# Both layers of a gated feed-forward block from split operands on the full array

## The chip, the cores and the metric

The kernel runs on one core of a Trainium2 chip. The metric is the device time of one execution in microseconds (us). One execution is also profiled: its trace gives the start and end of each instruction on the engines: TensorE (PE, with its weight loads PEld), VectorE (DVE), ScalarE (ACT), GpSimd (POOL), and the queues that issue DMAs (SP, and the queues of ACT and POOL).

## The reference

A causal convolution along the tokens with seven taps (the weights of a head, after a softmax over the taps, are shared by its 24 channels), then a feed-forward block with a hard-swish gate:

```python
B, S, D = 8, 4096, 192          # n_heads 8, kernel_size 7, d_ff 2048
w = softmax(weight, axis=-1)    # 8 x 7
x_pad = concatenate([zeros((B, 6, D)), x], axis=1)
y[b, s, h*24 + g] = sum_k w[h, k] * x_pad[b, s + k, h*24 + g]
h = y @ w_in                    # 32768 x 192 @ 192 x 2048
g = h * clip(h + 3, 0, 6) / 6
out = g @ w_out                 # 32768 x 2048 @ 2048 x 192
```

Both weight matrices arrive as 64-bit numbers and are rounded to fp32 on the chip. The input x arrives transposed, channels ahead of tokens.

## The kernel before, in words

The 32768 tokens are worked in 32 blocks of 1024, each as two halves of 512 tokens. d_ff is cut in 16 chunks of 128.

**Layout.** The 192 channels lie as three pieces (`K3`) of 64 rows. Partitions 0 to 63 hold the first 512 tokens of a block, 64 to 127 the second 512. A matmul of the first layer so uses half of the array's rows, and two of them, one per half, run side by side. w_in lies the same way, chunks 0 to 7 on the lower partitions and 8 to 15 on the upper ones. So that each token half also meets the other half's chunks, y is swapped between the partition halves by DMAs on SP (`swap`, `swap_parts`, L266/L267, six for each block).

**First layer.** Block 0 runs in plain fp32 (`half_mm`, L296). From block 1 on, `first_layer` (`mms`, L508 and L516) runs in the type float32r (f32r) on split operands: a number is cut by `high_of` and `from_high` into a high part and a rest, both short enough for that type, and a third part (MIX) that mixes both. For each of 16 (group, chunk) pairs it sums HIGH x HIGH and LOW x LOW in PSUM, has ACT multiply the sum by 4097 (L528), and adds MIX x MIX: 18 half-array matmuls of 512 columns, in nine pairs side by side. ACT's relu (L302) and DVE's gate (L306) then form g in SBUF.

**Second layer.** `second_layer` writes out a schedule by hand: four streams of matmuls, one per strip of 32 array columns, run side by side in fp32 (L623). It uses a seven-product scheme on 2 x 2 blocks (token half by d_ff half, d_ff half by output half), for one strip with a second level of the same scheme. This needs sums of parts of g: by DVE and POOL (`g_sums` L412, `small_sums` L586, L456), and by accumulating DMAs on POOL's queue (L565). Products are put together in PSUM and SBUF by ACT copies and DVE additions; DVE transposes 32 x 32 blocks (L462) and SP stores 32 columns at a time (L372, twelve DMAs of 64 KB a block).

**Side work.** `conv_jobs` does the taps of the block after next on ACT (first tap, L927) and DVE (L929), 1536 columns at a time; L474, L945 and L477 split y.

**Start.** `Rounding` turns 64-bit words into fp32 in units of 128 x 384: DVE takes exponent and mantissa out (`split`, L171, L175), ACT clamps (`clamp`, L183, L186, L189), DVE joins (`join`, L192, L196), POOL multiplies (L200). There are 16 units, eight for each layer. In block 0 they are interleaved with the first layer's relus and gates; the second layer of block 0 (`out_direct`, L341) runs as plain fp32 sums.

The order on each engine is the program's (`tc.manual_schedule()`); the semaphores follow from the tiles.

Of the kernel before, what the change touches and what calls it, by code (L numbers as in the profile page):

```python
# [18 lines left out]

CUT = 1.0 - 2.0**-13  # L20
EPS = 2.0**-12
HIGH, LOW, MIX = range(3)
# [3 lines left out]
def kernel(  # L26
# [17 lines left out]
    G = 2  # L44
    TB = G * N
    D2 = P // 2
    K3 = D // D2
    GJ = GS // K3
    NC = DFF // P
    NT = TB // P  # L50
    BPB = S // TB
    NB = B * BPB
    assert H * GJ == D2 and K3 * GJ == GS and G == 2 and S % TB == 0 and DFF % P == 0 and PAD <= N

    NP = NC // 2
    DH = D // 2
    QS = 32
    NQ = DH // QS
    assert NQ * QS == DH and NQ == 3 and P // QS == 4

    cst = ctx.enter_context(tc.tile_pool(name="cst", bufs=1))
    xs = ctx.enter_context(tc.tile_pool(name="xs", bufs=1))
    ys = ctx.enter_context(tc.tile_pool(name="ys", bufs=1))
    ot = ctx.enter_context(tc.tile_pool(name="ot", bufs=1))
    ps = ctx.enter_context(tc.tile_pool(name="ps", bufs=1, space=bass.MemoryType.PSUM))
    start_pools, first_in = ExitStack(), ExitStack()
    stg = start_pools.enter_context(tc.tile_pool(name="stg", bufs=8))
    cnv = start_pools.enter_context(tc.tile_pool(name="cnv", bufs=4))
    fi = first_in.enter_context(tc.tile_pool(name="fi", bufs=1, side="right"))

    def x_source(i):
        b, t0 = i // BPB, (i % BPB) * TB
        src = xT[b].rearrange("(p s) t -> p s t", s=K3)
        head = PAD if t0 == 0 else 0
        return head, src[..., t0 - PAD + head : t0 + N], src[..., t0 + N - PAD : t0 + TB]

    def load_x(i, dma=nc.sync):
        x = xs.tile([P, K3, PAD + N], F32, name="x")
        head, lower, upper = x_source(i)
        if head:  # L80
            nc.vector.memset(x[0:D2, :, 0:PAD], 0.0)
        dma.dma_start(out=x[0:D2, :, head:], in_=lower)
        dma.dma_start(out=x[D2:P, :, :], in_=upper)
        return x


    w_sb = cst.tile([P, KC], F32, name="w_sb")
    for base, dma in ((0, nc.scalar), (D2, nc.sync)):
        dma.dma_start(  # L89
            out=w_sb[base : base + D2],  # L90
            in_=weight.unsqueeze(1).to_broadcast([H, GJ, KC]),
        )


    x_tiles = {0: xs.tile([P, K3, PAD + N], F32, name="x")}
    nc.vector.memset(x_tiles[0][0:D2, :, 0:PAD], 0.0)

    def load_x0(s, dma_lower, dma_upper):
        head, lower, upper = x_source(0)
        dma_lower.dma_start(out=x_tiles[0][0:D2, s, head:], in_=lower[:, s])  # L100
        dma_upper.dma_start(out=x_tiles[0][D2:P, s, :], in_=upper[:, s])

    load_x0(K3 - 1, nc.gpsimd, nc.gpsimd)
    load_x0(0, nc.sync, nc.scalar)

# [4 lines left out]
    zeros = cnv.tile([P, N], F32, name="zeros", bufs=1)  # L110
    nc.vector.memset(zeros[:], 0.0)


    w_in = fi.tile([P, NP, K3, P], F32, name="w_in")


    w_out = cst.tile([P, NP, 7, DH], F32, name="w_out")
    B11, B12, B21, B22, T1, T2, T4 = range(7)
    T3 = B12
    w_s = cst.tile([P, 2, 4, NP // 2, QS], F32, name="w_s")  # L120

    w_in_bits = moe_w_in.bitcast(U32).rearrange("(p s) (c f w) -> c p s f w", s=K3, f=P, w=2)
    w_out_bits = moe_w_out.bitcast(U32).rearrange("(k c p) w -> p c k w", p=P, k=2)
    WS = K3 * P
    assert 2 * D == WS
# [4 lines left out]
    def load_w_in(j):  # L130
        st = stage()
        for half in range(2):
            nc.sync.dma_start(  # L133
                out=st[half * D2 : (half + 1) * D2].rearrange("p (s f) w -> p s (f w)", s=K3),
                in_=w_in_bits[j + half * NP].rearrange("p s f w -> p s (f w)"),
            )
        return st

    def load_w_out(j):
        st = stage()  # L140
        nc.sync.dma_start(
            out=st[:].rearrange("p (k d) w -> p k (d w)", k=2), in_=w_out_bits[:, j]
        )
        return st

# [5 lines left out]

    class Rounding:

        def __init__(self, load, dst):  # L160
            self.load_words, self.dst = load, dst

        def load(self):
            self.st = self.load_words()

        def split(self):
            high = self.st[:, :, 1]
            self.top = cnv.tile([P, WS], U32, name="top")
            self.scale = cnv.tile([P, WS], U32, name="scale")
            self.sig = cnv.tile([P, WS], F32, name="sig")  # L170
            nc.vector.tensor_scalar(  # L171
                out=self.scale[:], in0=high, scalar1=0x7FF00000, scalar2=None,
                op0=ALU.bitwise_and,
            )
            nc.vector.tensor_scalar(  # L175
                out=self.top[:], in0=high, scalar1=0xFFFFF, scalar2=0x100000,
                op0=ALU.bitwise_and, op1=ALU.bitwise_or,
            )

        def clamp(self):  # L180


            nc.scalar.activation(  # L183
                self.sig[:], self.scale[:], ACT.Relu, bias=bias_e[:, 0:1], scale=-1.0
            )
            nc.scalar.activation(  # L186
                self.scale[:], self.sig[:], ACT.Relu, bias=bias_e[:, 1:2], scale=-8.0
            )
            nc.scalar.mul(self.sig[:], self.st[:, :, 0], 2.0**-52)  # L189

        def join(self):
            nc.vector.scalar_tensor_tensor(  # L192
                out=self.scale[:], in0=self.st[:, :, 1], scalar=0x80000000,
                in1=self.scale[:], op0=ALU.bitwise_and, op1=ALU.bitwise_or,
            )
            nc.vector.scalar_tensor_tensor(  # L196
                out=self.sig[:], in0=self.top[:], scalar=2.0**-20, in1=self.sig[:],
# [3 lines left out]
                out=self.dst, in0=self.sig[:], in1=self.scale[:].bitcast(F32), op=ALU.mult  # L201
            )
    def w_in_unit(j):
        return Rounding(lambda: load_w_in(j), w_in[:, j].rearrange("p s f -> p (s f)"))

    def w_out_unit(j):
        dst = w_out[:, j, B11 : B22 + 1].rearrange("p b d -> p (b d)")
        return Rounding(lambda: load_w_out(j), dst)

    def w_sums(sums):  # L210
        for o, x, y in sums:
            nc.vector.tensor_tensor(
                out=w_out[:, :, o], in0=w_out[:, :, x], in1=w_out[:, :, y], op=ALU.subtract
            )

    units = [w_in_unit(j) for j in range(NP)] + [w_out_unit(j) for j in range(NP)]
    AHEAD = 4
    for n in range(AHEAD):
        units[n].load()
        if n == 0:  # L220
            load_x0(1, nc.sync, nc.sync)

    mx = cst.tile([P, 1], F32, name="mx")
    nc.vector.tensor_reduce(out=mx[:], in_=w_sb[:], axis=AX.X, op=ALU.max)
    e_sb = cst.tile([P, KC], F32, name="e_sb")
    nc.vector.tensor_tensor(
        out=e_sb[:], in0=w_sb[:], in1=mx[:].to_broadcast([P, KC]), op=ALU.subtract
    )
    nc.scalar.activation(e_sb[:], e_sb[:], ACT.Exp)
# [96 lines left out]

# [694 lines left out]
```

## Time and profile before

| what | us |
|---|---|
| three runs, median (lowest to highest) | 2230.66 (2230.26 to 2230.84) |
| span of the profiled execution, first to last instruction | 2228.3 |
| median less that span | 2.4 |
| TensorE busy | 2221.0 |
| DVE, ACT, POOL busy | 1894.3, 1379.2, 823.6 |
| fp32 matmuls of the second layer (L623) on g and w_out | 967.5 busy, 552 ns each |
| f32r matmuls of the first layer (L516), two groups | 524.9 and 516.1 busy, 388 and 386 ns each |
| gates (L306), 128 x 1024 | 598.0 busy, 1219 ns each |
| relus (L302), 128 x 1024 | 545.3 busy, 1113 ns each |

The profiled execution is known by its span; the three timed runs are other executions. Matmuls overlap, so the busy time of a group is less than count times mean, and a busy TensorE does not mean a full array. An fp32 matmul shows as two records (two passes), an f32r matmul as one. In the rows quoted below, `64*128` is rows by columns of the array that are in use, and the tile names say which operand is read.

### The profile page before, as it was taken

The page shows a single profiled execution, that of the slowest core. Times are in us where ns is not written, and L with a number is a line of the kernel's source. Part 1 is how long each engine was busy: PE and PEld are TensorE (multiplying, and loading weights), DVE is VectorE, ACT ScalarE, POOL GpSimd, SP SyncE. Part 2 cuts the span into 40 slices and gives each one's busy share as a digit, 9 for nine tenths or more (in the row PEclk, how much of TensorE's full clock was granted, in tenths as well). Part 3 has the DMA queues.
Part 4 walks back from the last instruction along what each step waited for, and adds up shares of the span by engine and source line. Part 5 has one row for each costly group of instructions (what it writes and reads, how often), then busy time and mean ns, then how long its engine had stood idle before and what let it go on. Part 6 is the DMA issues. An engine that isn't in the chain of part 4 may idle for free.

```text
span 2228.3 us, 50401 instructions
## 1 busy us (share of the span) xinstructions
PE 2221.0 (100%) x21527; PEld 1560.8 (70%) x21527; DVE 1894.3 (85%) x1673; ACT 1379.2 (62%) x1678; POOL 823.6 (37%) x690
## 2 busy tenths in 40 slices
PE   9999999999999999999999999999999999999999
PEld 5477776677766777766777667786677776677766
DVE  8888888888888888888888888888888888888876
ACT  7457665576655676555766557665567655576654
POOL 2344432344422444223443234442244422344323
PEclk9999999999999999999999999999999999999999
DMA  6244224443244342344422443324434234442232
GB/s 157 58 98 84 49 58 91 85 83 63 53 82 91 77 80 46 71 91 84 84 48 58 91 87 81 67 49 82 91 78 82 47 67 91 84 84 52 55 77 34
DMA packets 253584, 166.58 MB, mean 75 GB/s; under 512 B 208016, under 2 KB 213136, under 8 KB 253360
## 3 DMA queue, kind: packets, MB, share of 16 engines
q1 hardware_dynamic: 234872, 129.46, 28.4%
q0 software_dynamic: 17248, 33.64, 8.7%
q8 instruction: 169, 2.77, 0.5%
q10 hardware_dynamic: 1240, 0.27, 0.1%
q14 instruction: 55, 0.45, 0.1%
HBM read 31.72 MB, written 25.17 MB: 26 GB/s over the span
## 4 chain that ended last, share of the span: by engine, by line
PE 99%; DMA 0%; DVE 0%; SPq 0%; ACT 0%; issue 0%; DVEq 0%; ACTq 0%
PE psum L623 49%; PE psum L516 46%; PE psum L296 2%; PE psum L341 2%; PE psum L508 0%; DMA x<-in_x_dram 0%; SPq L100 0%; SPq L133 0%; DVE top L175 0%; PE psum L824 0%; DVE y L255 0%; DVE results L456 0%; SPq L89 0%; ACT y L838 0%; ACT scale L186 0%
## 5 line engine op out<-in xcount | busy, mean ns | idle before, releaser
L623 PE MATMUL psum<-g,w_out 128*32 128x512 f32 (+1 forms) x6712 | 967.5, 552 | 0.0
L306 DVE SCALAR_TENSOR_TENSOR g<-g,psum 128x1024 f32<-128x1024 f32 (+1 forms) x528 | 618.3, 1186 | 203.6 <-ACT g L302 203.1
L586 POOL TENSOR_TENSOR s<-g 128x256 f32<-128x256 f32 x248 | 273.9, 1104 | 1244.4 <-DVE g L306 1244.4
L302 ACT ACTIVATE g<-psum,half 128x1024 f32<-128x1024 f32 (+1 forms) x528 | 564.8, 1086 | 4.9 <-PE psum L516 0.3
L623 PEld LDWEIGHTS psum<-g,w_out 128*32 128x32 f32 x6712 | 371.7, 110 | 246.0 <-issue 126.7
L516 PE MATMUL psum<-y,w_in 64*128 64x512 f32 x4464 | 524.9, 388 | 0.0
L516 PE MATMUL psum<-y_other,w_in 64*128 64x512 f32 x4464 | 516.1, 386 | 0.0
L528 ACT ACTIVATE psum<-psum 128x1024 f32<-128x1024 f32 x465 | 469.0, 1009 | 54.4 <-PE psum L516 52.1
L516 PEld LDWEIGHTS psum<-y,w_in 64*128 64x128 f32 x4464 | 435.4, 184 | 71.2 <-ACT psum L528 0.3
L516 PEld LDWEIGHTS psum<-y_other,w_in 64*128 64x128 f32 x4464 | 423.8, 184 | 82.1
L623 PE MATMUL psum<-s,w_out 128*32 128x512 f32 (+1 forms) x3272 | 465.5, 570 | 0.0
L929 DVE SCALAR_TENSOR_TENSOR y<-x,c_sb,y 128x1536 f32<-128x1536 f32 x186 | 335.3, 1803 | 2.6 <-ACT y L927 1.4
L412 POOL TENSOR_TENSOR s<-g 128x1024 f32<-128x1024 f32 x93 | 285.8, 3073 | 26.7 <-DVE g L306 26.5
L623 PE MATMUL psum<-g,w_s 128*32 128x256 f32 x1240 | 282.8, 379 | 0.0
L623 PEld LDWEIGHTS psum<-s,w_out 128*32 128x32 f32 x3272 | 154.3, 110 | 81.8 <-issue 49.4
L623 PEld LDWEIGHTS psum<-g,w_s 128*32 128x32 f32 x1240 | 136.4, 110 | 67.7
L412 DVE TENSOR_TENSOR s<-g 128x2048 f32<-128x2048 f32 (+1 forms) x93 | 181.3, 1977 | 1.1
L623 PE MATMUL psum<-s,w_s 128*32 128x256 f32 x744 | 170.7, 379 | 0.0
L586 DVE TENSOR_TENSOR g<-g 128x1024 f32<-128x1024 f32 x124 | 151.7, 1224 | 5.2
L412 DVE TENSOR_TENSOR g<-g 128x2048 f32<-128x2048 f32 x62 | 139.0, 2284 | 0.0
L620 ACT COPY psum<-psum 32x512 f32<-32x512 f32 x93 | 51.3, 551 | 135.4 <-PE psum L623 135.4
L456 DVE TENSOR_TENSOR results<-psum,results 32x256 f32<-32x256 f32 (+3 forms) x128 | 69.3, 541 | 50.9 <-issue 45.5
(93 smaller groups left out, 1316.6 us busy)
## 6 DMA issues: line engine op xcount, KB each, us to landing
y_other<-y SPq DMA_DIRECT2D x186, 384.0 KB, 5.1
g<-g POOLq DMA_DIRECT2D x62, 512.0 KB, 5.0
out_dram<-results SPq DMA_DIRECT2D x378, 64.0 KB, 2.0
x<-in_x_dram SPq DMA_DIRECT2D x53, 388.5 KB, 7.7
stage<-in_moe_w_in_dram SPq DMA_DIRECT2D x16, 192.0 KB, 4.8
stage<-in_moe_w_out_dram SPq DMA_DIRECT2D x8, 384.0 KB, 5.5
x<-in_x_dram SPq DMA_DIRECT2D x7, 384.0 KB, 8.3
x<-in_x_dram POOLq DMA_DIRECT2D x2, 388.5 KB, 5.3
```

The source lines that it names most:

```text
L296: nc.tensor.matmul(out=psum[:, b], lhsT=w[r], rhs=src, start=start, stop=stop, skip_group_check=onto,)
L302: nc.scalar.activation(r6, h, ACT.Relu, bias=half[:], scale=1.0 / 6.0)
L306: nc.vector.scalar_tensor_tensor(out=g_, in0=g_, scalar=1.0, in1=h, op0=ALU.min, op1=ALU.mult)
L341: lambda p=p: nc.tensor.matmul(out=bank[j * QS : (j + 1) * QS, tokens], lhsT=w_out[:, p, w, cols], rhs=x[:, p, tokens], start=(first and p ...
L412: engine.tensor_tensor(out=o[:, r], in0=a[:, r], in1=b[:, r], op=op)
L456: nc.vector.tensor_tensor(out=out, in0=x, in1=y, op=op)
L516: nc.tensor.matmul(out=psum[:, 2 * slots[n] + k], lhsT=r32(w_in_parts[part][r, c, s]), rhs=r32(y_other[0][r, part, s] if group else y_own[ ...
L528: nc.scalar.mul(both(n), both(n), 4097.0)
L586: engine.tensor_tensor(out=o, in0=p, in1=q, op=op)
L620: streams[3].append((t - 0.5, lambda: fn(*args, **kw)))
L623: nc.tensor.matmul(out=out, lhsT=w, rhs=x, start=start, stop=True, tile_position=(0, j * QS), skip_group_check=True,)
L929: jobs.append(lambda k=k: nc.vector.scalar_tensor_tensor(out=y[:], in0=x[:, :, k : k + N], scalar=c_sb[:, k : k + 1], in1=y[:], op0=ALU.mu ...
```

## The change

Both layers now run in f32r on operands split in two parts that this type holds exactly, a high part and the rest, with all products summed straight in PSUM. There is no scaling between the products, no seven-product scheme, and no fp32 matmul but seven for the convolution of block 0.

- Layout: 128 of the 192 channels (16 of each head) fill all partitions for 1024 tokens (part a). The other 64 channels (part b) lie in both partition halves, one token half each.
- First layer of a chunk: for part b, high x low weight on half the rows, two side by side (`first_rows`); then four full-array matmuls per token half (`first`): part b's high and low parts stacked on 128 rows, and part a's high x high, high x low weight, low x full weight.
- Second layer of a chunk (`second`): three products on g's high part and two on its low part, for each token half: ten full-array matmuls. One of them holds 64 columns of high weights and 64 of low ones, so that its two row halves are added at the store.
- Order: chunks go in pairs. In each block TensorE does the first layer of pair p, then the second layer of pair p - 1. After relu and gate, ACT copies g's high part and DVE subtracts it for the low part.
- Start: sixteen units, of 512 columns for the first layer and 384 for the second. Besides the rounding, each also makes high and low parts (`parts_of`, ACT and POOL). The two units of pair p + 1 are placed behind pair p's work in block 0.
- Gone: the swaps of y, the sums of g, the accumulating DMAs, and the additions between products.

The diff, cut to the core of the new code:

```diff
+    def parts_of(sig, high, lows):
+        nc.scalar.mul(r32(high), sig, CUT)
+        for to, src, top in lows:
+            nc.gpsimd.tensor_tensor(out=r32(to), in0=src, in1=top, op=ALU.subtract)
+
+    def in_unit(j):
+        high, low = (w1[:, n, j].rearrange("p a c f -> p (a c f)") for n in range(2))
+
+        def finish(sig):
+            parts_of(sig, high, [(low, sig, high)])
+            nc.scalar.copy(
+                out=r32(w1_full[:, j].rearrange("p c f -> p (c f)")), in_=sig[:, 0 : 2 * P]
+            )
+            nc.scalar.copy(out=r32(high[D2:P, 2 * P :]), in_=sig[D2:P, 2 * P :])
...
+    def matmul(out, w, x, start, stop, position=(0, 0)):
+        nc.tensor.matmul(
+            out=out, lhsT=r32(w), rhs=r32(x), start=start, stop=stop,
+            tile_position=position, skip_group_check=True,
+        )
+
+    def first_rows(c, yp):
+        for k, b in enumerate(banks_of(c)):
+            matmul(
+                psum[:, b], w1[rows[k], LOW, c // 2, 1, c % 2], yp[3][rows[k]],
+                True, False, (k * D2, 0),
+            )
+
+    def first(c, yp):
...
+        steps = (
+            (w1[:, HIGH, c // 2, 1, c % 2], 2), (w1[:, HIGH, c // 2, 0, c % 2], HIGH),
+            (w1[:, LOW, c // 2, 0, c % 2], HIGH), (w1_full[:, c // 2, c % 2], LOW),
+        )
+        for k, b in enumerate(banks_of(c)):
+            for n, (w, x) in enumerate(steps):
+                matmul(psum[:, b], w, yp[x][:, halves[k]], False, n == len(steps) - 1)
+
+    def second(p, parts):
...
+        for c in range(2):
+            w = w2[:, 2 * p + c]
+            jobs += [(0, w[:, 0], high, c), (0, w[:, 2], high, c), (2, w[:, 1], high, c)]
+        for c in range(2):
+            ch = 2 * p + c
+            jobs += [(0, w2_full[:, ch], low, c), (2, w2[:, ch, 1], low, c)]
...
+    def store(i):
...
+        for k in range(2):
+            nc.scalar.copy(out=upper[rows[k]], in_=psum[rows[1 - k], SUMS + 2 + k])
+        xts = [ot.tile([P, N], F32, name="xt") for _ in range(3)]
+        for k in range(2):
+            nc.vector.transpose(out=xts[k][:], in_=psum[:, SUMS + k])
+        for k in range(2):
+            nc.vector.tensor_tensor(
+                out=sums[rows[k]], in0=psum[rows[k], SUMS + 2 + k], in1=upper[rows[k]],
+                op=ALU.add,
+            )
+        nc.vector.transpose(out=xts[2][:], in_=sums[:])
...
+    def unit_step(n):
+        if n < len(units):
+            units[n].split()
+            units[n].clamp()
+            units[n].join()
+            units[n].part()
+        if n + AHEAD < len(units):
+            units[n + AHEAD].load(nc.sync)
...
+            for p in range(NP):
+                parts = new_g()
+                pair = 2 * p, 2 * p + 1
+                for c in pair:
+                    first_rows(c, yp)
+                for c in pair:
+                    first(c, yp)
+                if finished is not None:
+                    store(finished)
+                    finished = None
+                for c in pair:
+                    relu_of(c, parts)
+                for c in pair:
+                    gate_of(c, parts)
+                for c in pair:
+                    g_high(c, parts)
+                for c in pair:
+                    g_low(c, parts, nc.vector)
+                if last is not None:
+                    second(*last)
+                    if last[0] == NP - 1:
+                        finished = i - 1
+                last = p, parts
+                if i == 0:
+                    unit_step(2 * p + 2)
+                    unit_step(2 * p + 3)
...
+                if more:
+                    if p == 0:
+                        tap(xn, 0, 0, nc.scalar)
+                        tap(xn, 1, 0, nc.scalar)
+                    for part, k in taps[2 * p : 2 * p + 2]:
+                        tap(xn, part, k, nc.vector)
+                    if p == NP - 2:
+                        yn = new_y()
+                        split_a(yn)
+                        split_b(yn)
```

In the changed kernel the helper's matmuls stand at L309 and L310, the copy that waits for POOL at L209, the relu at L360, the gate at L368, the high part at L374, the low part at L378, and the store's DMAs at L384.

## The prediction

> **What bounds the kernel now.** I read the page's busy shares and its chain first, then stages (busy time by windows), then the order in time on TensorE inside one block, then single groups by shape, then the start.
>
> The page:
> ```profile
> span 2228.3 us, 50401 instructions
> PE 2221.0 (100%) x21527; PEld 1560.8 (70%) x21527; DVE 1894.3 (85%) x1673; ACT 1379.2 (62%) x1678; POOL 823.6 (37%) x690
> ...
> PE 99%; DMA 0%; DVE 0%; SPq 0%; ACT 0%; issue 0%; DVEq 0%; ACTq 0%
> PE psum L623 49%; PE psum L516 46%; PE psum L296 2%; PE psum L341 2%; PE psum L508 0%; DMA x<-in_x_dram 0%; SPq L100 0%; SPq L133 0%; DVE top L175 0%; PE psum L824 0%; DVE y L255 0%; DVE results L456 0%; SPq L89 0%; ACT y L838 0%; ACT scale L186 0%
> ```
> TensorE is the whole chain: the second layer (L623) 49%, the first (L516) 46%. Only matmul slots, or a stall that opens between them, can move the time.
>
> Stages (columns: window, its length, busy time of PE, PEld, DVE, ACT, POOL, granted clock, DMA share, GB/s):
> ```profile
> 0.00:99.70 99.70, 97.64 (x600) 44.76 (x600) 87.95 (x149) 61.10 (x98) 29.44 (x34) 1.00 0.43 101
> 99.70:168.20 68.50, 68.50 (x677) 53.46 (x673) 58.65 (x48) 42.09 (x50) 27.07 (x22) 1.00 0.52 107
> 1058.50:1127.00 68.50, 68.50 (x674) 48.55 (x673) 59.02 (x49) 42.64 (x51) 25.64 (x21) 1.00 0.38 74
> ```
> Block 0 lasts 99.7 us, then come 31 blocks of 68.49 (L508 starts every block), and 5.4 at the end: 99.7 + 2123.2 + 5.4 = 2228.3. The clock is 1.00 throughout.
>
> TensorE in order of time (start, length):
> ```profile
> 1058.56 0.38 PE L508 MATMUL psum<-y,w_in 64*128 64x256 f32 x1
> 1058.57 16.09 PE L516 MATMUL psum<-y,w_in 64*128 64x512 f32 x138
> 1074.49 1.52 PE L516 MATMUL psum<-y_other,w_in 64*128 64x512 f32 x12
> ...
> 1076.53 15.12 PE L516 MATMUL psum<-y_other,w_in 64*128 64x512 f32 x132
> 1091.58 6.64 PE L623 MATMUL psum<-g,w_out 128*32 128x512 f32 x63
> ```
> The first layer takes 33.0 us, the second 35.5. The 66 pairs of half-array f32r matmuls in the x132 row take 15.12 - 0.16 = 14.96 us: **226.7 ns a pair**. (One record lasts 386 ns, 0.16 us beyond the next pair's start.)
>
> Two other spacings, an fp32 pass of 256 columns and the full array in fp32:
> ```profile
> 2222.06 0.38 PE L623 MATMUL psum<-g,w_out 128*32 128x256 f32 x1
> 2222.27 0.38 PE L623 MATMUL psum<-g,w_out 128*32 128x256 f32 x1
> 2222.49 0.38 PE L623 MATMUL psum<-g,w_out 128*32 128x256 f32 x1
> ```
> ```profile
> 6.17 7.14 PE L824 MATMUL psum<-x,diag 128*128 128x512 f32 x16
> ```
> A 256-column pass comes every 0.215 to 0.216 us; a 512-column pass on the full array every 0.43 (7.14 less a tail of 0.59 and a first gap of 0.53, over 14).
>
> The price of the weight conversion:
> ```profile
> 9.98 0.60 ACT L183 ACTIVATE sig<-scale,bias_e 128x384 f32<-128x384 uint32 x1
> 10.61 0.62 ACT L186 ACTIVATE scale<-sig,bias_e 128x384 uint32<-128x384 f32 x1
> 11.26 0.56 ACT L189 ACTIVATE sig<-stage 128x384 f32<-128x384 uint32 x1
> 11.86 0.56 DVE L196 SCALAR_TENSOR_TENSOR sig<-top,sig 128x384 f32<-128x384 uint32 x1
> 12.50 1.04 POOL L200 TENSOR_TENSOR w_in<-sig,scale 128x384 f32<-128x384 f32 x1 [9.40 <-DVE sig L196]
> ```
> One unit is a chain through ACT, DVE and POOL. Hand-overs cost 0.03 to 0.08 us.
>
> **The change, part by part.**
>
> *Matmul slots.* Gone: 144 f32r pairs (33.0 us) and seven-product sums in fp32 (35.5 us). New, for each of 8 pairs of d_ff chunks: the first layer is 2 concurrent row pairs and 16 full-array f32r matmuls, 18 slots; the second is 20. That is 304 slots a block, no fp32 pass. No row shows f32r on the full array. Bounds: 216 ns (half of an fp32 pass of 512 columns, all of one of 256) and 226.7 (the pair's period). I take 223.3: the nearest row by type is f32r, and its second matmul starts 3.3 ns after the first, so 223.4 pass from one pair's last start to the next pair. 288 x 0.2233 + 16 x 0.2267 = **67.9 us a block**, against 68.5.
>
> *What must hide.* In a pair TensorE does F(p), 4.03 us, then S(p-1), 4.47. F(p+1) needs both gates of p: after F(p) ends, 0.25 + relu 1.11 (L302) + gate 1.22 (L306) = 2.6 us, under the 4.47 of S. S(p) wants the high parts (ACT copy, 1.05, from L474's 1479 for 1536 columns) and the low ones (DVE subtraction, 1.22, from L456) a pair later. DVE per block: 32 x 1.22 + taps 6 x 1.27 + 6 x 0.74 + y split 2.6 + transposes 3 x 0.70 + sums 1.4 = 57 us; ACT: 16 x (1.11 + 1.05) + 5.9 = 40. Both fit. At a block's second pair the store's transposes and sums sit ahead of the gates: taps end 2.4 us into F(1), the sums 4.9, and S(0) first writes the last bank at 5.1. Stall 0 to 0.3 us; I take 0, since the gates then end 0.7 us before F(2). The removed swaps (6 DMAs of SP a block), accumulating DMAs (2 of POOL's queue) and POOL sums were all off the chain: worth nothing. SP issues 12 stores and 3 x loads a block, 15 x 0.6 = 9 us of 68, and each x load has a block's lead. 31 x 67.9 = 2106.
>
> *Block 0.* Both layers' converted weights are now needed pair by pair, and the program places the units behind the pair's gates in each queue, ahead of the next pair's relu. The chain of a pair, scaling 384 columns to 512 for the wider unit (ACT +0.11, DVE +0.14, POOL x 4/3):
> - first-layer unit: DVE 0.44; ACT 0.73 + 0.73 + 0.68; DVE 0.69; POOL 1.45; ACT high part 0.58; POOL low part 1.45; ACT copy that waits for it 0.36: 7.1.
> - second-layer unit, its ACT steps queued behind that copy: 0.62 + 0.62 + 0.57, DVE 0.55, POOL 1.06, ACT 0.48 + 0.37: 4.3.
> - relu 2 x 1.11 (queued behind those), gate 1.22, high 1.05, low 1.22: 5.7.
>
> That copy (L209) is a new wait of ACT on POOL: the second unit's clamps and the next pair's relu stand behind it, and DVE's gates behind the relu. With some 14 hand-overs, 17.9 us a pair against 8.5 of TensorE. The start: words land near 10 us (the queues already move some 220 GB/s there before), unit 0 and seven taps of 1024 columns end near 20, the split y near 25, unit 1's ACT part near 30, the first pair's low parts near 36. Six more pairs, the first with 1.8 of ACT taps in front of the relu: 36 + 6 x 17.9 + 1.8 = 145. Then the last units (12.0), the y split on ACT (2.6) and the last pair's relu and gate (2.4) let block 1 start at **162**; 1 for a TensorE that idles long between bursts and restarts at half clock (its first, idle-started fp32 passes came 853 ns apart, later 429): 163. Before: 99.7. So **+63 us**. Bounds: 115 if the engines filled each other's waits (11 us of DVE a pair), 180 if hand-overs and POOL run a tenth slower.
>
> *End.* S(7) 4.5, transposes 1.0, twelve stores issued by SP alone at 0.58 each (six take 3.50 in the end of before), landing 2: 14.4 against 5.4. Bounds 11 to 16.
>
> *Sum.* 163 + 2106 + 14.4 = 2283.4 of span; 2.4 us lie between the profiled span and the median (2230.66 - 2228.3): **2286 us**, 2.5% slower. 0.2% (4.5 us) is about what this kernel's runs can tell.
>
> **The rivals.**
> 1. *Full-array f32r has no extra gap*: 216 ns a slot as the fp32 rows have it. Block 65.7 + 0.2 of store stall; 163 + 31 x 65.9 + 14.4 + 2.4 = 2223, faster by 0.3%. The turning point is (2230.7 - 179.8) / 31 / 304 = 217.6 ns. For it: the gap beyond 216 shows on pairs alone. Against: in fp32, pairs (L296) and full array (L824) keep the same 429 ns, so pairing cost nothing there. The Trainium skill (TensorE: Matmul & The Clock Gate, Part 1) gives 215.7 ns start to start for 512 columns when warm; by it the sum, an estimate, would be 2220. The fp32 rows agree with that fixed part, the f32r pair does not.
> 2. *The slot is 226.7 or more*, or each F's row pairs start spread out, as the first pairs of a layer do here. 68.9 a block gives 2316; with 0.11 us for each of 8 F stages, 2343. For it: 226.7 is the period that f32r has here.
> 3. *Block 0 overlaps*: at 115 us the time is 2238. Against: ACT and DVE take their queues in order.
> 4. *Weights are not hidden*: each full-array matmul waits for its load. The exposed load at the first fp32 pass was 0.53 - 0.43 = 0.10 us; 288 x 0.10 x 31 = 893 us more, about 3180. Against: later L824 loads begin with the pass before and cost nothing. The Trainium skill (same page, Part 3, on what overlaps) says a weight load overlaps a running matmul only where its row group differs. That rule speaks against this change; L824 contradicts it here.
>
> **How the numbers follow.** Forecast 0.52, rival 1 0.22, rival 2 0.18, rival 3 0.06, rival 4 0.02. The likeliest case gives 2286 (its own range 2270 to 2300, from block 0 and the end). Rival 1 with an uncertain block 0 is faster two times in three, within 0.2% one in five: faster 0.16, same 0.06, slower 0.78. Range 2212 (rival 1, block 0 ten us shorter) to 2335 (inside rival 2).
>
> **What would show it.** The starts of successive full-array matmuls (223 or 216); block 1's first matmul near 163; gaps of TensorE before L309's row matmuls in block 0 released by ACT, DVE and POOL work of the units; no gap over 0.3 us later; DVE near 57 us and ACT near 40 a block; twelve stores in a row on SP at the end. The prediction fails if the slot lies below 217.6 ns, or if block 0 ends well before 150.

## The result, and the profile after

| | before | after |
|---|---|---|
| median of the timed runs, us | 2230.73 | **2478.24** (2477.30 to 2478.47) |
| ratio, 95% interval | | **1.1109** (1.1093 to 1.1125) |
| span of the profiled execution | 2228.3 | 2476.0 |
| block 0 (to block 1's first first-layer matmul) | 99.7 | 172.5 |
| each of the 31 later blocks | 68.49 | 73.87 |
| the end, behind the last of these blocks | 5.4 | 13.6 |

The change makes the kernel 11.1% slower. The forecast was slower by 2.5%, 2286 us, and its range ended at 2335: the sign was right, the size was not. 172.5 + 31 x 73.87 + 13.6 = 2476.1 is the whole span, so the three terms of the forecast can be held against it one by one: block 0 +9.5 us, the end -0.8, and the blocks 31 x (73.87 - 67.9) = **+185**. Nearly all of the miss lies in the block. There the sign was wrong too: the forecast had each block 0.6 us shorter than before (67.9 against 68.49), and it is 5.4 us longer. The forecast's "slower" came from block 0 and the end alone.

The page of the changed kernel (busy time, then the chain of work that ended last, by engine, then its costliest groups):
```profile
span 2476.0 us, 25270 instructions
PE 2391.4 (97%) x10254; PEld 1808.1 (73%) x10254; DVE 1803.8 (73%) x1750; ACT 1309.3 (53%) x1376; POOL 47.6 (2%) x51
...
PE 94%; DVE 2%; ACT 2%; POOL 1%; DMA 1%; issue 1%; ACTq 0%; DVEq 0%; SPq 0%
...
L360 ACT ACTIVATE g<-psum,half 128x1024 f32<-128x1024 f32 x512 | 572.2, 1118 | 968.7 <-PE psum L309 968.7
L368 DVE SCALAR_TENSOR_TENSOR g<-g,psum 128x1024 f32<-128x1024 f32 x512 | 622.2, 1221 | 602.2 <-ACT g L360 601.2
L309 PE MATMUL psum<-high,w 128*128 128x512 f32 x3072 | 756.7, 395 | 0.0
```
TensorE is still the bound. ACT idles 969 us for TensorE and DVE 601 for ACT, while the second layer's group has no idle time in front of it. So no engine took TensorE's place, and nothing that had to hide came out; the matmuls themselves are dearer.

Stages (window, its length, busy time of PE, PEld, DVE, ACT, POOL where it worked, granted clock, DMA share, GB/s):
```profile
0.00:172.50 172.50, 96.78 (x314) 67.73 (x314) 104.20 (x133) 91.88 (x140) 47.63 (x51) 0.79 0.21 61
172.50:246.37 73.87, 73.87 (x321) 56.01 (x320) 57.07 (x54) 40.27 (x41) 0.00 (x0) 1.00 0.11 22
1058.50:1132.37 73.87, 73.87 (x322) 56.03 (x321) 55.08 (x53) 39.34 (x40) 0.00 (x0) 1.00 0.11 22
```
In block 0 TensorE is busy for 96.8 of 172.5 us and its granted clock is 0.79. Later the clock is 1.00, DVE works 55 to 57 us and ACT 40 in a block (forecast 57 and 40), and TensorE is busy throughout.

One pair of d_ff chunks on TensorE in order of time (start, length; rows join neighbours of one kind):
```profile
1068.17 0.73 PE L309 MATMUL psum<-yb_high,w 64*128 64x512 f32 x4
1068.83 0.50 PE L309 MATMUL psum<-yb,w 128*128 128x512 f32 x1
1069.17 0.62 PE L309 MATMUL psum<-ya_high,w 128*128 128x512 f32 x2
1069.63 0.40 PE L309 MATMUL psum<-ya_low,w_full 128*128 128x512 f32 x1
...
1072.65 2.96 PE L309 MATMUL psum<-high,w 128*128 128x512 f32 x12
1075.45 0.62 PE L309 MATMUL psum<-low,w_full 128*128 128x512 f32 x2
...
1077.40 0.73 PE L309 MATMUL psum<-yb_high,w 64*128 64x512 f32 x4
```
A pair takes 9.23 us. The four row-tile matmuls, two slots, take 0.66 us until the next kind starts, and twelve full-array matmuls 2.80: 233 ns each. From the starts of single matmuls, averaged over some 50 pairs:

| gap between starts, ns | after |
|---|---|
| two row tiles of one concurrent pair | 3 to 4 |
| row pair 1 to row pair 2 | 332 |
| row pair 2 to the first full-array matmul | 324 |
| first to second full-array matmul | 339 |
| the next 34, full array to full array | 228 to 241, a pattern that repeats every seven; mean of the 34 232.5, of whole sevens 232.4 |
| last full-array matmul to the next row pair | 327 |

Two things are dearer than the 223.3 ns of the forecast: every slot by 9 ns, and the four gaps around the two changes of tile (into the row pairs and out of them) by 0.1 us each. 304 x 9.1 = 2.8 us a block and 32 x 0.1 = 3.2 make up the 6.

### The profile page after: what moved, and what is told of

It is laid out like the page before. It is cut to its first block, busy times and chain, and to the rows that moved or that the text cites. A ratio compares the mean times of both kernels' runs of the same rounds, so it can differ in the third digit from the quotient of the medians.

```text
span 2476.0 us, 25270 instructions
## 1 busy us (share of the span) xinstructions
PE 2391.4 (97%) x10254; PEld 1808.1 (73%) x10254; DVE 1803.8 (73%) x1750; ACT 1309.3 (53%) x1376; POOL 47.6 (2%) x51
## 3 DMA queue, kind: packets, MB, share of 16 engines
q8 instruction: 80, 1.31, 0.2%
q0 software_dynamic: 592, 1.06, 0.2%
## 4 chain that ended last, share of the span: by engine, by line
PE 94%; DVE 2%; ACT 2%; POOL 1%; DMA 1%; issue 1%; ACTq 0%; DVEq 0%; SPq 0%
PE psum L309 94%; POOL sig L189 1%; DVE g L368 0%; DMA w_sb<-in_weight_dram 0%; POOL w L199 0%; DVE sig L185 0%; ACT sig L172 0%; ACT scale L175 0%; DVE y L279 0%; DVE low L378 0%; ACT w L197 0%; DMA x<-in_x_dram 0%; ACT g L360 0%; ACT sig L178 0%; DVE scale L181 0%
## 5 line engine op out<-in xcount | busy, mean ns | idle before, releaser
L360 ACT ACTIVATE g<-psum,half 128x1024 f32<-128x1024 f32 x512 | 572.2, 1118 | 968.7 <-PE psum L309 968.7
L368 DVE SCALAR_TENSOR_TENSOR g<-g,psum 128x1024 f32<-128x1024 f32 x512 | 622.2, 1221 | 602.2 <-ACT g L360 601.2
L309 PE MATMUL psum<-high,w 128*128 128x512 f32 x3072 | 756.7, 395 | 0.0
L309 PEld LDWEIGHTS psum<-high,w 128*128 128x128 f32 x3072 | 579.1, 188 | 135.5
L309 PE MATMUL psum<-ya_high,w 128*128 128x512 f32 x2048 | 650.0, 399 | 1.0 <-ACT ya_high L303 1.0
L378 DVE TENSOR_TENSOR low<-g,high 128x1024 fp32r<-128x1024 f32 x512 | 619.6, 1223 | 0.0
L374 ACT CAST high<-g 128x1024 fp32r<-128x1024 f32 x512 | 535.5, 1046 | 105.4 <-DVE g L368 102.8
L309 PEld LDWEIGHTS psum<-ya_high,w 128*128 128x128 f32 x2048 | 391.0, 191 | 82.4 <-ACT ya_high L303 1.3
L309 PE MATMUL psum<-yb,w 128*128 128x512 f32 x1024 | 435.7, 426 | 0.0
L309 PE MATMUL psum<-ya_low,w_full 128*128 128x512 f32 x1024 | 408.3, 399 | 0.0
L309 PE MATMUL psum<-low,w 128*128 128x512 f32 x1024 | 323.8, 397 | 0.0
L309 PE MATMUL psum<-low,w_full 128*128 128x512 f32 x1024 | 318.9, 392 | 0.0
L309 PEld LDWEIGHTS psum<-yb,w 128*128 128x128 f32 x1024 | 195.7, 191 | 131.6 <-issue 90.7
L309 PE MATMUL psum<-yb_high,w 64*128 64x512 f32 x1024 | 191.1, 451 | 56.6 <-POOL w L199 55.0
L309 PEld LDWEIGHTS psum<-ya_low,w_full 128*128 128x128 f32 x1024 | 195.8, 191 | 45.5 <-DVE ya_low L304 0.8
L309 PEld LDWEIGHTS psum<-low,w_full 128*128 128x128 f32 x1024 | 193.4, 189 | 46.2
L309 PEld LDWEIGHTS psum<-low,w 128*128 128x128 f32 x1024 | 192.3, 188 | 43.7
L309 PEld LDWEIGHTS psum<-yb_high,w 64*128 64x128 f32 x1024 | 77.7, 188 | 151.3 <-issue 81.9
```

The costliest lines, as they stand in the source:

```text
L309: nc.tensor.matmul(out=out, lhsT=r32(w), rhs=r32(x), start=start, stop=stop, tile_position=position, skip_group_check=True,)
L360: nc.scalar.activation(parts[2][c % 2][:], psum[:, b : b + 2].rearrange("p k n -> p (k n)"), ACT.Relu, bias=half[:], scale=1.0 / 6.0,)
L368: nc.vector.scalar_tensor_tensor(out=g, in0=g, scalar=1.0, in1=psum[:, b : b + 2].rearrange("p k n -> p (k n)"), op0=ALU.min, op1=ALU.mult,)
L374: nc.scalar.copy(out=r32(parts[HIGH][:, c % 2]), in_=parts[2][c % 2][:])
L378: engine.tensor_tensor(out=r32(low), in0=parts[2][c % 2][:], in1=high, op=ALU.subtract)
```

## The experiments

The theories are numbered as they arose. 1: f32r on the full array has a longer slot of its own. 2: going over between half-row tiles and full-array tiles costs. 3: block 0 is set by the units' place in the queues. 4: matmuls have two settled patterns, and an exposed load starts the slow one. 5 and 6: the place of the operands in SBUF. Every run is compared with the kernel before on the same chip. The code of the stream runs is shortened here.

### Bare streams of matmuls

All of the kernel's work is replaced by runs of 64 matmuls each, varying type and tile, and runs that alternate between tiles:

```diff
+for i in range(64):   # f32r, full array; likewise bf16, half rows, 256 columns
+    nc.tensor.matmul(out=psum[:, i % 8], lhsT=r32(wr[:, i % NW]), rhs=r32(xs(xr, i)), start=i < 8, **kw)
+for j in range(8):    # eight on the full array, then two row pairs; likewise bf16
+    for i in range(8): nc.tensor.matmul(out=psum[:, j % 4], lhsT=r32(wr[:, i]), ...)
+    for i in range(2):
+        for k in range(2): nc.tensor.matmul(..., lhsT=r32(wr[rows[k], i]), tile_position=(k * D2, 0), ...)
```


> Bare streams of 64 matmuls of one kind each, 512 columns, no other engine at work: the convolution, both layers and the gate are left out, the output is zeros. Theory 1 (the price lies in the f32r matmul on the full array itself): full array f32r starts every 232 ns, on one bank or on changing banks; half-row pairs 227; bf16 full array 216. Rival (the changed kernel's 232 comes from the other engines' traffic or from waits): full array f32r 216 to 223 here. Theory 2 (a change between full-array and half-row tiles drains the array, 0.2 us each): eight full and two row pairs take 10 slots and 0.4 us, 2.7 us, in f32r and as much over the slots in bf16 and fp32. Rival (changes are free, the gaps of the changed kernel are semaphore waits at the start of a pair): 10 slots, 2.3 us.

TensorE in order of time: f32r full array (L87), bf16 full array (L94), f32r with 256 columns (L100), then the alternation in f32r (L111 full, L114 row pairs) and bf16 (L118, L121):
```profile
34.33 14.67 PE L87 MATMUL psum<-xr,wr 128*128 128x512 f32 x64
...
63.91 13.76 PE L94 MATMUL psum<-xb,wb 128*128 128x512 bf16 x62 [0.16 <-issue]
...
92.36 7.93 PE L100 MATMUL psum<-xr,wr 128*128 128x256 f32 x64
...
131.47 2.12 PE L111 MATMUL psum<-xr,wr 128*128 128x512 f32 x8
133.52 0.73 PE L114 MATMUL psum<-xr,wr 64*128 64x512 f32 x4
134.18 2.12 PE L111 MATMUL psum<-xr,wr 128*128 128x512 f32 x8
...
155.16 1.90 PE L118 MATMUL psum<-xb,wb 128*128 128x512 bf16 x8
157.00 0.60 PE L121 MATMUL psum<-xb,wb 64*128 64x512 bf16 x4
157.53 1.90 PE L118 MATMUL psum<-xb,wb 128*128 128x512 bf16 x8
```
Start to start, settled: f32r on the full array **226.7 ns** (14.67 less a tail of 0.39, over 63), the same as row pairs and half rows alone; bf16 215.8. So the gap beyond 216 belongs to the type f32r, not to the pairing, and rival 1 of the prediction is out. The alternation has a cycle of 134.18 - 131.47 = 2.71 us, where ten slots are 2.27: **0.44 us for going to row tiles and back**. In bf16 it is 2.37 against 2.16: 0.21. In fp32 (same run, not shown) a cycle costs 0.40 us over its slots. Theory 2 holds for f32r and fp32; for bf16 it expected as much, and half came. Theory 1 expected 232 ns and its rival 216 to 223; both missed, and 5.7 ns a slot between the streams' 226.7 and the kernel's 232.4 stayed open.

### No row tiles

The part-b high operand is padded with zeros, so that the row matmuls use all 128 rows: 40 slots instead of 38, and no change of tile.

```diff
-                psum[:, b], w1[rows[k], LOW, c // 2, 1, c % 2], yp[3][rows[k]],
-                True, False, (k * D2, 0),
+                psum[:, b], w1[:, LOW, c // 2, 1, c % 2], yp[3][:, k], True, False,
```


> The low-weight product of part b on all 128 rows, with zeros in the other token half's rows, instead of two half-row matmuls side by side: 40 slots a pair of chunks instead of 38, and no change of tile shape. Theory 2 (0.2 us per change, 16 changes a block): 40 x 0.2324 = 9.30 us a pair against 9.23, block 74.4, time 2490 to 2500. Rival (changes are free): 9.23 + 2 x 0.232 = 9.70 a pair, block 77.6, time near 2594.

2495.04 us, ratio 1.1188 (1.1169 to 1.1206). The low-weight product (now L313, on all rows) of two pairs in a row:
```profile
1065.84 1.09 PE L313 MATMUL psum<-yb_high,w 128*128 128x512 f32 x4
...
1075.13 1.08 PE L313 MATMUL psum<-yb_high,w 128*128 128x512 f32 x4
```
Over 30 blocks a pair takes 9.297 us. 40 x 232.4 ns = 9.296: with no change of tile a pair is nothing but slots, and the pattern of seven runs on without a break. Two slots more (0.465 us) make the pair only 0.06 us longer than the changed kernel's, so the changes of tile cost 0.40 us a pair. It also shows that the 232.4 has nothing to do with the changes.

### What block 0 waits for

In one run the units are rounded one pair ahead, only the parts are made in front of their pair, and the copy that waits for POOL comes last:

```diff
-                    unit_step(2 * p + 2)
-                    unit_step(2 * p + 3)
+                    part_pair(2 * p + 2)             # parts of units rounded a pair earlier
+                    prepare((2 * p + 4, 2 * p + 5))  # split, clamp, join, loads
```


> The weight units are rounded one pair ahead of where their high and low parts are made, so that in block 0 no ACT step waits for POOL between a pair's low parts and the next relu. If the chain of the units sets block 0 (theory 3): about 11 us a pair instead of 18 to 19, block 1 starts near 120 instead of 172.5, time near 2428. Rival (block 0 is held by the landing of the words or by the sums of DVE or ACT work): block 1 starts after 155 and the time stays above 2460.

2447.15 us, ratio 1.0974 (1.0958 to 1.0990). The first row matmuls (now L312) of two pairs of block 0:
```profile
103.90 1.22 PE L312 MATMUL psum<-yb_high,w 64*128 64x512 f32 x4 [4.67 <-POOL w L200]
...
117.90 0.73 PE L312 MATMUL psum<-yb_high,w 64*128 64x512 f32 x4 [2.22 <-POOL w L200]
```
Pairs of block 0 follow each other every 14.0 us instead of 18.8, and block 1 starts at 143.3 instead of 172.5. Later blocks keep 73.87. The direction was right; the gain was 31 us where 50 were expected.

In another the conversion is left out altogether:

```diff
-            units[n].split()
-            units[n].clamp()
-            units[n].join()
+            units[n].sig = units[n].temporary("sig")
+            nc.vector.tensor_copy(out=units[n].sig, in_=units[n].words(1).bitcast(F32))
```


> The changed kernel with the conversion of the 64-bit weights left out (split, clamp and join: 3 DVE, 3 ACT and 1 POOL instruction of 384 or 512 columns a unit); one DVE copy of one half of the words stands in its place, so the sums are not the reference's. The parts (ACT high, POOL low, ACT copies) stay. Theory 3 (block 0 is the chain of unit work ahead of the next pair's relu): without the conversion a pair's two units shrink from some 11.4 us of chain to POOL 1.45 + 1.06 and ACT 0.58 + 0.36 + 0.5 + 0.4 plus two copies of 0.4, about 5 us; pairs of block 0 start about 11 to 13 us apart instead of 18.9, block 1 starts at 115 to 130 instead of 172.5, the span is 2418 to 2434; later blocks stay at 73.87. Rival (block 0 is set by the loads of weights, or by the taps, gates and parts of the products): block 1 starts above 150. If the later blocks change, the data or the units bear on the 232.4 ns slot, which neither theory has.

2444.17 us in one run; block 1 starts at 138.9, above the 115 to 130 expected, and pairs come every 13.9 us. In time, on all engines, that run shows what is left between two first layers:
```profile
65.20 2.95 PE L309 MATMUL psum<-high,w 128*128 128x512 f32 x12
65.40 1.12 ACT L360 ACTIVATE g<-psum,half 128x1024 f32<-128x1024 f32 x1 [1.07 <-PE psum L309]
...
66.55 1.22 DVE L368 SCALAR_TENSOR_TENSOR g<-g,psum 128x1024 f32<-128x1024 f32 x1 [0.97 <-ACT g L360]
67.69 2.42 DVE L378 TENSOR_TENSOR low<-g,high 128x1024 fp32r<-128x1024 f32 x2
...
70.03 0.69 DVE L410 COPY sig<-stage 128x512 f32<-128x512 f32 x2
...
70.48 0.63 ACT L197 ACTIVATE w<-sig 128x512 fp32r<-128x512 f32 x1 [1.63 <-DVE sig L410]
...
71.19 1.84 POOL L199 TENSOR_TENSOR w<-sig,w 128x512 fp32r<-128x512 f32 x1 [9.85 <-ACT w L197]
...
73.09 0.73 PE L309 MATMUL psum<-yb_high,w 64*128 64x512 f32 x4 [3.08 <-POOL w L199]
```
Pair p's second relu ends at 66.5, its gate at 67.8, its low parts at 70.1. Only then does DVE's queue reach the unit's work, and the next first layer, at 73.09, waits for POOL's low weight. The conversion is worth 5 us of a pair of 18.8; the other 14 are this loop through the first layer, relu, gate, low parts and weight parts, in one order on every queue. The first layer is its largest part: from 59.18 to the second layer's start at 65.20 it takes 6.0 us, at a mean granted clock of 0.72, where a later block's takes 4.5 at 1.00, and both relus wait for it. In the changed kernel itself only the second relu does, for 0.34 us at 75.16. With the conversion a pair ahead the pairs are 14.0 us apart too, but not for this reason alone: first layers of 4.5 us (from 89.92) and of 7.0 us (from 103.90, at a granted clock of 0.60) are followed by the same 14.0. So block 0 is not a chain of units alone.

### Why 232.4 and not 226.7

First, restarts and the other engines. The streams begin behind fp32, behind row pairs, behind bf16 and out of idle, and once with DVE and ACT at work:

```diff
+pairs(2)                                  # or four fp32, or one bf16, or a wait for DVE
+for i in range(128): full(i, i % 4)       # full-array f32r
+for i in range(12):                       # ahead of the last stream only
+    nc.scalar.copy(out=r32(xh[:]), in_=src[:, 0:1024])
+    nc.vector.tensor_tensor(out=r32(xg2[:]), in0=src[:, 0:1024], in1=src[:, 1024:2048], op=ALU.subtract)
```


> Bare streams again (no convolution, no layers, the output is no result): what turns the 226.7 ns of a full-array f32r stream into the 232 ns of the changed kernel. Theory 4 (the spacing has two settled patterns, and a weight load exposed by a change of tile shape starts the slower one): behind fp32 226.7; behind half-row pairs 231 to 232 for all 128 matmuls; behind four fp32 matmuls 226.7 again; behind one bf16 matmul 226.7 or 231, which tells whether a bf16 matmul is enough to mend it; from idle 231 to 232, since the first load is exposed there too. Rival (traffic of the other engines): behind pairs and from idle it falls back to 226.7 within some ten matmuls, and the last 80, with DVE and ACT at work, take 230 or more.

The stream behind row pairs, 128 matmuls, as one row:
```profile
35.73 29.32 PE L83 MATMUL psum<-xr,wr 128*128 128x512 f32 x128
```
After a first longer gap, each stream has two to eight gaps of 224 to 236 ns and then stays at 226.7, whatever came before it. In the last stream DVE and ACT both work beside some 45 of the matmuls, and the gap stays 226.7. Theory 4 fell. Its rival had the fall back to 226.7 right, but the other engines' traffic, its cause for the 232, changes nothing.

Then the operands themselves, in nine streams of 40:

```diff
+lhsT=r32(wr[:, i % NW]),  rhs=r32(xs(xr, i))      # A near; E, F, G reuse weights, operand, bank
+lhsT=r32(wr[:, i % NW]),  rhs=r32(xs(xfar, i))    # B far; I further
+lhsT=r32(w64[:, i % NW]), rhs=r32(xs(x64, i))     # C far, both shifted; D near, both shifted
```


> All of the computation is left out (the output is zeros); nine streams of 40 f32r matmuls on the full array, 128 rows, 128 weight columns, 512 columns, one fp32 matmul between them (about 0.4 us). Open: the changed kernel's full-array slots are 232.4 ns start to start in a pattern that repeats every seven, bare streams settle at 226.7. Stages in order: A weights near the moving operand; B moving operand 84 KB further per partition; C as B, weights and moving operand both shifted by 64 bytes; D near, both shifted by 64 bytes; E each weight used twice in a row; F each moving operand used four times in a row; G all 40 summed in one bank; H as the second layer of the changed kernel (each weight twice, weights with a stride of three, sums in two banks, moving operand far); I moving operand another 60 KB further. Theory 5a, addresses: one or more of B, C, D, I stays near 232 over the whole stage (40 slots: 9.3 us) and A, E, F, G at 226.7 (9.07 us). Theory 5b, the way operands and banks repeat: E, F, G or H stays near 232 and B, C, D, I at 226.7. Rival: all nine settle at 226.7 after at most nine slots (9.07 to 9.12 us each); then the 5.7 ns come from something that only the whole kernel has, and stay open.

Stages B and C as rows:
```profile
30.70 9.89 PE L107 MATMUL psum<-xfar,wr 128*128 128x512 f32 x40
...
40.89 9.65 PE L111 MATMUL psum<-x,w 128*128 128x512 f32 x40
```
Means of the last 20 gaps: A 226.6, **B 233.3**, C 226.6, D 226.7, E 226.6, F 226.6, G 226.7, H 228.7, **I 232.4**. Reuse, banks and sums do nothing; the place of an operand does. I has the changed kernel's own pattern (230, 233, 241, 232, 231, 232, 228). But C is far away too (68 KB, B 84 KB) and stays at 226.6, so it is not the distance as such. What B and I share is the distance from weights to moving operand, modulo 256 bytes: 128, where it is 0 in A, C and D, and 64 in H. Worked out from the order and sizes of the tiles in the programs (no trace holds an address), it is 0 for the f32r pairs of the kernel before, and 128 for all operands of the changed kernel.

The next stream run varies nothing else:

```diff
+for offset in (0, 32, 64, 96, 128, 160, 192, 224, 256):   # bytes; then far away 0, 64, 128, 192
+    for i in range(40):
+        at = offset // 4 + (i % 2) * N
+        nc.tensor.matmul(out=psum[:, i % 4], lhsT=r32(wr[:, i % NW]), rhs=r32(x[:, at : at + N]), ...)
```


> All of the computation is left out (the output is zeros). Thirteen streams of 40 f32r matmuls on the full array (128 rows, 128 weight columns, 512 columns, weights and two halves of a moving operand in turn), one fp32 matmul between them. Only the place of the moving operand in SBUF changes: the distance from the weights' first byte to its own, modulo 256 bytes, is in stages 1 to 9 (24 KB away) 64, 96, 128, 160, 192, 224, 0, 32, 64, and in stages 10 to 13 (111 KB away) 64, 128, 192, 0. Theory 6: this distance modulo 256 sets the settled slot. It was 0 in the streams that settled at 226.7 ns and in the kernel before, 128 in the changed kernel (232.4) and in stages B and I of the stream run before (233.3, 232.4), 64 in its stage H (228.7). So the stages at 0 settle at 226.7 (40 slots with restart 9.1 us), those at 128 at 232 to 233 (9.3), those at 64 and 192 between; 24 KB or 111 KB away makes no difference. Rival 6b, the distance itself: stages 1 to 9 all settle at 226.7 and 10 to 13 at 232 or more. If some distance settles near 216 as bf16 does, the 226.7 is a matter of addresses too, which neither has.

| distance modulo 256 bytes | 0 | 32 | 64 | 96 | 128 | 160 | 192 | 224 |
|---|---|---|---|---|---|---|---|---|
| settled gap, ns, 24 KB away | **226.6** | 233.3 | 228.8 | 233.1 | 232.6 | 234.4 | 233.4 | 233.4 |
| about 110 KB away | **226.6** | | 228.8 | | 233.3 | | 233.4 | |

In order of time (stages at 128, 0, and far away at 128 and 0):
```profile
39.91 9.85 PE L98 MATMUL psum<-xo,wr 128*128 128x512 f32 x40
...
80.65 9.64 PE L98 MATMUL psum<-xo,wr 128*128 128x512 f32 x40
...
120.83 9.90 PE L98 MATMUL psum<-xf,wr 128*128 128x512 f32 x40
...
141.21 9.68 PE L98 MATMUL psum<-xf,wr 128*128 128x512 f32 x40
```
Of the eight distances only 0 gives 226.6, near or far. None comes close to bf16's 216.

The same in the changed kernel, with 128 unused bytes per partition behind the weights:

```diff
     w2_full = cst.tile([P, NC, P], F32, name="w2_full")
+    shift = cst.tile([P, 32], F32, name="shift")
+    nc.vector.memset(shift[:], 0.0)
```


> The changed kernel with 128 unused bytes per partition between the weights and everything behind them, so that every moving operand lies 0 instead of 128 bytes from its weights modulo 256. Nothing else changes. Theory 6 (the address decides): the 35 full-array gaps of a pair that average 232.4 ns go to 226.7 after a restart of some nine at 231 behind the change of tile: pair 9.03 to 9.08 us instead of 9.233, block 72.3 to 72.7, whole 2426 to 2440 us; the four long gaps at the changes (0.32 to 0.34 us) stay. Rival 6b (distance, or something of the whole kernel): pair stays at 9.23, 2474 to 2480.

**2433.41 us**, ratio 1.0909 (1.0893 to 1.0926): 44.8 us less than the changed kernel, from one unused tile. The same stretch of a pair as above (the matmul's line is now L311):
```profile
1068.12 0.50 PE L311 MATMUL psum<-yb,w 128*128 128x512 f32 x1
...
1071.88 2.88 PE L311 MATMUL psum<-high,w 128*128 128x512 f32 x12
1074.61 0.62 PE L311 MATMUL psum<-low,w_full 128*128 128x512 f32 x2
...
1076.51 0.73 PE L311 MATMUL psum<-yb_high,w 64*128 64x512 f32 x4
1077.17 0.50 PE L311 MATMUL psum<-yb,w 128*128 128x512 f32 x1
```
Twelve matmuls now take 2.73 us, 227 ns each; a pair 9.05, a block 72.43. The four gaps around the changes of tile stay: 332, 323, 338, 318. Theory 6 holds in the kernel, at the size that the streams gave.

Last, both improvements together (units a pair ahead, and the unused tile):

> The changed kernel with units rounded one pair ahead (as in the run of that change, 2447.15) and with the 128 unused bytes. By theory 6 both gains add, since one lies in block 0 and the other in all later blocks: 2447 less 31 blocks of 1.2 to 1.6, that is 2397 to 2410 us; block 1 starts near 142. Still slower than the kernel before, since a pair has 36 full-array slots of 226.7 and four changes of tile of some 0.33. Rival 6b: 2444 to 2450.

2402.04 us, ratio 1.0767 (1.0749 to 1.0785); block 1 starts at 143.1, blocks take 72.43. The two gains add. It remains 7.7% slower than the kernel before, and no run points to a form of this change that would pass it: with block 0 as short as before, 31 blocks of 72.43 are still 122 us more than 31 of 68.49, and 304 bare slots of 226.7 ns are already 68.9 us.

## Why the prediction was wrong

**The slot was mis-sized, in two parts.** The step said "I take 223.3: the nearest row by type is f32r, and its second matmul starts 3.3 ns after the first, so 223.4 pass from one pair's last start to the next pair". The row was the right one, the deduction from it wrong: the period of the pair, 226.7, is what f32r takes on the full array too. That is 3.4 ns on 288 slots, 1.0 us a block, 30 us in all. It was the upper bound of that step, and rival 2 gave 2316 by it. The second part is the address: 232.4 instead of 226.7, worth 73.87 - 72.43 = 1.44 us a block, 45 in all. No row of the trace before could show it, since its f32r pairs lie at distance 0.

**The change of tile was priced at nothing.** The forecast counted "2 concurrent row pairs and 16 full-array f32r matmuls, 18 slots", as if rows of both kinds followed each other at the pace of one kind. Only rival 2 had a price, 0.11 us for each first layer. Without the address, a block takes 72.43 where 304 slots of 226.7 are 68.92: the changes of tile cost **3.5 us a block, 109 in all**, the largest term of the miss. The bare alternation gives the same to 0.01 us: 38 x 0.2267 + 0.44 = 9.05 a pair. The profile of the changed kernel shows what it is (weight loads and matmuls around a change, start and length):
```profile
1067.61 0.63 PE L309 MATMUL psum<-low,w 128*128 128x512 f32 x2
1067.61 0.19 PEld L309 LDWEIGHTS psum<-low,w 128*128 128x128 f32 x1
1068.17 0.30 PEld L309 LDWEIGHTS psum<-yb_high,w 64*128 64x128 f32 x4 [0.37 <-issue]
1068.17 0.73 PE L309 MATMUL psum<-yb_high,w 64*128 64x512 f32 x4
...
1068.83 0.19 PEld L309 LDWEIGHTS psum<-yb,w 128*128 128x128 f32 x1 [0.36 <-issue]
1068.83 0.50 PE L309 MATMUL psum<-yb,w 128*128 128x512 f32 x1
1068.94 0.42 PEld L309 LDWEIGHTS psum<-ya_high,w 128*128 128x128 f32 x2
```
Between matmuls of one shape the load of the next weights runs beside the matmul before it (1067.61, both). At a change of shape the load side idles for 0.37 and 0.36 us, for nothing that the profile shows. The load starts at 1068.17, 0.33 us after the last full-array matmul did (1067.84), and the new shape's first matmul starts with it.

Single starts in the bare alternations split the price in two. The load for the new shape starts some 0.09 us later than the next slot would, in f32r, fp32 and bf16 alike. Then the second matmul of the new shape comes 0.10 to 0.11 us late in f32r and fp32, whose loads take 182 to 190 ns, and 0.01 us late in bf16, where they take 92 to 98. So the second half goes with the length of the exposed load; 0.10 us is also what rival 4 had read off the first fp32 pass. What holds the load back in the first half the runs do not show, and no run varied the load by itself.

**Rival 4 was right at the places where the shape changes.** Between full-array matmuls of one shape the 188 ns of the load are wholly hidden inside 226.7. Between the half-row tiles and the full array, in f32r and in bf16, the load is not pulled ahead. The prediction dismissed the rival for the first reason and never asked of the second. The Trainium skill (TensorE: Matmul & The Clock Gate, Part 3, on what overlaps) says that a weight load overlaps a running matmul only where its row group differs. The measurement differs from it for matmuls of one shape, which have one row group; at the changes, where the two shapes share rows, it agrees if "differs" means that no row is shared. The Trainium skill's 215.7 ns for 512 columns (same page, Part 1) agrees with bf16 (215.8) and not with f32r (226.7), both at a granted clock of 1.00.

**Block 0** was forecast to end at 163 and ended at 172.5. The larger part of the 9.5 us lies at the start: the first pair's low parts, forecast near 36, ended at 41.9. There DVE stood until 13.49 waiting for the convolution's weights to land (until 4.23 in the kernel before), and unit 0's POOL product over 512 columns took 2.23 us instead of 1.45, beside a DVE tap. The next six pairs took 112.7 us, where 109.2 were forecast (the chain of 17.9 us a pair was 18.8), and the last stretch 18.0, as forecast. One term of the chain that was short is visible in the trace of the changed kernel:
```profile
70.80 2.69 DVE L279 SCALAR_TENSOR_TENSOR y<-x,c_sb,y 128x1024 f32<-128x1024 f32 x2
70.96 1.98 POOL L189 TENSOR_TENSOR sig<-sig,scale 128x384 f32<-128x384 f32 x1 [3.04 <-DVE sig L185]
...
83.29 1.31 POOL L189 TENSOR_TENSOR sig<-sig,scale 128x512 f32<-128x512 f32 x1 [8.56 <-DVE sig L185]
83.40 1.42 DVE L166 TENSOR_SCALAR top<-stage 128x384 uint32<-128x384 uint32 x1
```
POOL's product over 384 columns, counted with 1.06 us, takes 1.98 where it starts beside a DVE tap (1.01 at 164.33, where no tap runs); the 512 columns take 1.31 where POOL comes first, and then it is DVE's work that takes longer, 1.42 us. The 0.9 us is as much as the chain was short; the chain also left out the wait of the second relu for TensorE (0.34 us here). The two runs on block 0 correct its description too: the chain's sum was nearly right, but the conversion is only 5 us of it, and neither run came near the lower bound of 115.

**What was right.** TensorE stays the bound; the gates, relus, high and low parts, stores and taps all hide (DVE 57, ACT 40 us a block, no wait after block 0); the end, with twelve stores in a row on SP, took 13.6 against 14.4; and rival 3, an overlapping block 0, did not come. "No gap over 0.3 us later" holds for idle time, since TensorE is busy in all of a later block; it did not catch the miss, because the changes of tile show only in the distances between starts, four of 0.32 to 0.34 in each pair. The right sign is in part luck: the forecast drew it from block 0 and the end, which give 81 of the 247.7 us by which the span grew; the blocks, forecast to gain 18, give the other 167.

The sum, closed: 31 x (1.0 for the type + 3.5 for the tiles + 1.44 for the address) is 184; with 9.5 for block 0 and -0.8 for the end it is 193, and the span differs from the forecast by 2476.0 - 2283.4 = 192.6.

## What to carry to other kernels

Count matmul slots by the period that the type shows, not by a difference of starts inside it, and give every change between half-row and full-array tiles its own price: some 0.22 us in f32r and 0.11 in bf16 here. For back-to-back f32r matmuls look at the addresses: a multiple of 256 bytes between weights and moving operand kept the slot at 226.7 ns, six of the seven other distances tried gave 232.6 to 234.4, and one unused tile won 1.8%. A new chain at the start of a kernel is to be read as a loop through all queues; shortening one part of it gives back only until the next part of the loop sets the pace.

## What the runs showed of the hardware that was not expected

- f32r matmuls of 512 columns come every 226.7 ns on the full array, in row pairs and on half the rows alone, while bf16 takes 215.8; with 256 columns f32r takes 120.0, and with only 64 weight columns 230.0 (means of the last 20 gaps).
- The settled gap of f32r depends on the distance of its two operands in SBUF modulo 256 bytes, by up to 8 ns, near or about 110 KB away. What inside the chip does this, the runs do not show.
- A weight load is not pulled ahead across a change between half-row and full-array tiles (the load side idles 0.36 us). After such a change, or any other restart tried, f32r streams at distance 0 have two to nine gaps of 224 to 236 ns before the slot settles.
- POOL and DVE, started together on SBUF operands, took longer than alone: 1.98 us for POOL's 384 columns beside a tap (1.01 alone), 1.42 for a DVE operation over 384 columns (L166) that takes 0.35 alone.
- In block 0 of the changed kernel, where TensorE idles between bursts, its granted clock was 0.79; a first layer took 7.0 us there (from 67.97, clock 0.60) and 4.5 later at 1.00.
